# Moving score tile 0 out of the shared score banks, and wider planning margins, in a planned attention + FFN kernel

## The chip, the cores and the metric

The kernel runs on one core of one Trainium2 chip. The metric is the device time of one execution in microseconds, less is better. The kernel before takes 1138.29 us (median of 3 runs, 1138.12 to 1141.94).

## The reference

Attention over 8 batches x 8 heads, 576 positions, head dimension 64, with a block-causal mask (blocks of 64: a query sees all keys of its own block and the blocks before it). Its output, put together to 4608 tokens x 512 features, goes through a bilinear FFN without a nonlinearity:

```
scores = where(block(i) >= block(j), q @ k.T / sqrt(D), -1e9)
attn   = softmax(scores);  x = (attn @ v) as [4608, 512]
out    = ((x @ w_a) * (x @ w_b)) @ w_out          # d_ff = 1536
```

All is float32. The kernel gets float32 accuracy out of cheaper products by splitting each operand into a high and a low part and adding three products.

## The kernel before, in words

**The work.** Two heads make a pair, there are 32 pairs (four a batch). Pairs 0 to 9 multiply in plain float32, pairs 10 to 31 with split operands. Of 576 query rows the first 64 join the last 64 in a side tile, the other 512 make four tiles of 128 rows (0 to 3), which see 192, 320, 448 and 512 keys in the products. For each pair the chain is:

- TensorE, scores: C3 (tile 3), C1 (the side tile, then tile 1), C2 (tile 2), C0 (tile 0), at L542. Head 0 lies on partitions 0 to 63, head 1 on 64 to 127, and their products run at the same time.
- VectorE: masking by memset (L576 to L580), the rows' maxima (t3, t4, t1, t2, t0, L568); ScalarE: the exponentials with their sums (e3, e4, e1, e2, e0, one instruction a head, L595).
- VectorE takes the reciprocals (rc), GpSimd multiplies (N, L683), VectorE transposes in blocks of 32 (T, L688) and sixteen DMAs put these in place (D, L739). Pairs 0 to 5 transpose on TensorE instead.
- TensorE multiplies with v: V, 60 matmuls in four steps (L748), into the output sums' bank, and its first 64 columns into a second bank (`av0`). ScalarE copies the sums out (X, L766 and L767), splits them (H, L787), GpSimd makes the low part (S, L791).

When the four pairs of a batch are done, the batch's tokens can go through the FFN, in two halves of 288 tokens each. A half takes 8 groups `ps` of 12 matmuls (L261) for the two first products of four of the twelve slices of d_ff, and 4 groups `pso` of 12 for the output; ScalarE or VectorE empties each group's bank (copy L837, product L841, copy L873). The rest of d_ff is done in later passes with other code (L1160), which takes from about 560 us to the end and has TensorE alone.

**PSUM.** Eight banks: `x` has two (tiles 3 and 2 of a pair, one bank a head), `y` has two (tile 1 with the side tile, then tile 0), `av` one (the output sums), and `mm` is a ring of three that the FFN's groups, `av0` and a few others take in turn (MM = 3): whoever takes a bank waits until the holder three places before it has released it.

**The order.** All instructions of the attention stage are first listed as operations (`Op`, L365) with an engine, an estimated duration, dependencies and a priority key. `plan` (L376) simulates the five engines and writes their instruction streams in the planned order. So an order is fixed when the program is built, and on the chip each engine works through its stream in that order. Attention's operations have keys near their pair's base time, FFN groups have key 1e6: they fill TensorE whenever no attention operation is ready, in pieces of four matmuls. Two constants matter here. Changing between the three kinds of TensorE work (mode 0 FFN, 1 scores, 2 output) is charged SWITCH = 0.1 us (L406). A TensorE operation that needs another engine's result is planned SLACK = 0.3 us after that result's estimated end (L417). Ring banks are followed by `since` (L391) with the holder's planned release and no such margin.

**Around the change.** C3 of a pair waits for e2 of the pair before (bank x), C1 for e0 of the pair before (bank y). C2 follows e3 (bank x), C0 follows C2, e1 and e4 (bank y). V of pair p-2 is made to follow C0 of pair p and then has key 0, ahead of all else (L776 to L780). D of pair p waits for V of pair p-2, which frees the buffer. Pair 0 alone (`single`) already puts its tiles 0 and 2 into ring and output banks.

Of the kernel before, what the change touches and what calls it, by code (L numbers as in the profile page):

```python
# [17 lines left out]
P = 128  # L18
# [12 lines left out]
KB = {"lk": 288, "lq": 320, "lv": 320, "cd": 512, "D": 112, "st": 144, "xd": 288}  # L31
RATE, LATENCY = 250.0, 1.9
SLACK = 0.3
MASKED = 1
SINGLE = 1
K2 = 2
# [6 lines left out]
CONV_KEY = 12.0  # L43
CONV_LO = True
KEEP_UNTIL, KEEP_EVERY = 66.0, 2.5
SWITCH = 0.1
LAGS = {"PE": 0.24, "DVE": 0.14, "Activation": 0.17, "Pool": 0.1, "SP": 2.0}
TOOK = {
# [31 lines left out]
}  # L80
EARLY = 5
# [8 lines left out]
def attention_then_bilinear_ffn(  # L90
# [274 lines left out]
    class Op:  # L365

        def __init__(self, kind, eng, fn, deps=(), at=0.0, key=None, mode=0):
            self.kind = kind
            took, lag, also = TOOK[kind]
            self.eng, self.took, self.fn, self.also, self.mode = eng, took, fn, also, mode  # L370
            self.deps = [d if isinstance(d, tuple) else (d, 0.0) for d in deps if d is not None]
            self.at, self.key, self.lag = at, at if key is None else key, lag
            self.n, self.frees, self.end = len(ops), None, None
            ops.append(self)

    def plan(look=0.0):  # L376
        free = dict.fromkeys(LAGS, 0.0)
        ready = {e: [] for e in LAGS}
        users = [[] for _ in ops]
        left = [len(o.deps) for o in ops]  # L380
        for o in ops:
            for d, plus in o.deps:
                users[d.n].append((o, plus))
            if not o.deps:
                ready[o.eng].append(o)
        out = []
        mode = 0
        bus = 0.0
        held = []

        def since(o):  # L391
            if not o.frees:
                return o.at
            if len(held) < MM:
                return o.at
            r = held[-MM]
            return o.at if r is o else 1e9 if r.end is None else max(o.at, r.end)

        while any(ready.values()):
            t, e = min((max(free[e], min(map(since, q))), e) for e, q in ready.items() if q)  # L400
            o = min((o for o in ready[e] if since(o) <= t + look), key=lambda o: (o.key, o.n))
            t = max(t, since(o))
            if o.frees:
                held.append(o.frees)
            ready[e].remove(o)
            free[e] = t + o.took + (SWITCH if e == PE_ and o.mode != mode else 0)  # L406
            if e == PE_:
                mode = o.mode
            if o.also:
                free[ACT_] = max(free[ACT_], t) + o.also  # L410
            o.start, o.end = t, free[e] + o.lag
            if o.kind in KB:
                bus = max(bus, t + LATENCY - 0.3) + KB[o.kind] / RATE
                o.end = bus + 0.3
            out.append(o)
            for u, plus in users[o.n]:
                u.at = max(u.at, o.end + plus + (SLACK if u.eng == PE_ and e != PE_ else 0))  # L417
                left[u.n] -= 1
                if not left[u.n]:
                    ready[u.eng].append(u)  # L420
        assert len(out) == len(ops)
        return out
# [37 lines left out]
    def got(what, p):  # L460
        return done.get((what, p))

    def attention(p):
# [11 lines left out]
        def add(what, eng, fn, deps=(), off=0.0, kind=None, **kw):  # L475
            deps = [(got(*d[:2]), *d[2:]) if isinstance(d, tuple) else (d,) for d in deps]
            done[what, p] = o = Op(kind or what, eng, fn, [(*d, 0.0)[:2] for d in deps if d[0]], key=B0 + off, **kw)
            return o

        add("lk", SP_, lambda: take(p, "k", S, kT[b, h0:h0 + 2].rearrange("h d s -> (h d) s")),  # L480
# [42 lines left out]
        def bank(x):  # L523
            st[x] = ps_sc.tile([P, 2, 512], F32, tag=x, name=f"{x}{n}_{len(st)}")
            return st[x]

        single = p < SINGLE

        def ring(t, h):
            st[t, h] = ps_mm.tile([P, 512], F32, tag="mm", name=f"s{n}_{t}_{h}")  # L530

        def view(t, h):
            if single and t in (0, 2):
                return st[t, h][:, :nk[t]]
            return st["x" if t in (2, LAST) else "y"][:, h, :nk[t]]

        def scores(t, out):
            qk = products(p, heads[p]["q"], heads[p]["k"])
            for j, (qq, kk) in enumerate(qk):
                for h, r in enumerate(rows):  # L540
                    keys = ends(kk[r]) if t == NT else kk[r, :nk[t]]
                    nc.tensor.matmul(  # L542
                        out[h] if isinstance(out, list) else out[:, h], qq[r, q0[t]:q0[t] + P], keys, start=j == 0,
                        stop=j == len(qk) - 1 and not (masked and t != LAST), skip_group_check=masked)
            if masked and t != LAST:
                for h, r in enumerate(rows):
                    to = out[h] if isinstance(out, list) else out[:, h]
                    to, val = (to, neg[r]) if t == NT else (to[:, nk[t] - BLK:nk[t]], neg[r, BLK:])
                    nc.tensor.matmul(to, who[r], val, start=False, stop=True, skip_group_check=True)
# [4 lines left out]

        def c1():
            y = bank("y")
            scores(NT, y[:, :, side])
            scores(1, y[:, :, :nk[1]])

        add("C3", PE_, lambda: scores(LAST, bank("x")), [("ql", p), ("kl", p), ("e3" if single_next else "e2", p - 1)], 0, at=B0, mode=1, kind=nat + "C3")  # L560
        add("C1", PE_, c1, [("C3", p, -LAGS[PE_]), ("ql2", p), *([("e4", p - 1), ("e1", p - 1)] if single_next else [("e0", p - 1)])], 0.1, mode=1, kind=nat + "C1")

        def tile_small():
            st["nm"], st["rc"] = (apool.tile([P, 2, NT + 1], F32, tag=x, name=f"{x}{n}") for x in ("nm", "rc"))
# [52 lines left out]
        exp_pair(NT, [("nb", p)], 4.5)  # L617
        exp_pair(1, [("t1", p)], 5.5)

        if single:  # L620
            c1_ = ("C1", p, -LAGS[PE_])
            r2 = Op("none", PE_, lambda: ring(2, 0), [(got("C1", p), -LAGS[PE_])], key=B0 + K2)

            def c2():
                ring(2, 1)
                scores(2, [view(2, h) for h in range(2)])

            o2 = add("C2", PE_, c2, [(r2, 0.0), c1_], K2 + .01, mode=1, kind=nat + "C2")
            def c0():
                ring(0, 1)  # L630
                st[0, 0] = ps_sc.tile([P, 512], F32, tag="av", name=f"s{n}_0_0")
                scores(0, [view(0, h) for h in range(2)])

            o0 = add("C0", PE_, c0, [("C2", p, -LAGS[PE_]), ("X", p - 1)], K2 + .1, mode=1, kind=nat + "C0")
            add("t2", DVE_, lambda: [nc.vector.tensor_reduce(st["nm"][:, h, 2:3], view(2, h), axis=AX.X, op=ALU.max, negate=True) for h in range(2)], [("C2", p), ("t3", p)], K2 + 1, kind="u2")
            add("t0", DVE_, lambda: [nc.vector.tensor_reduce(st["nm"][:, h, :1], view(0, h), axis=AX.X, op=ALU.max, negate=True) for h in range(2)], [("C0", p), ("t3", p)], K2 + 1.2, kind="u0")
        else:
            add("C2", PE_, lambda: scores(2, bank("x")[:, :, :nk[2]]), [("e3", p), ("C1", p, -LAGS[PE_])], 7.0, mode=1, kind=nat + "C2")
            add("C0", PE_, lambda: scores(0, bank("y")[:, :, :nk[0]]),
                [("C2", p, -LAGS[PE_]), ("e1", p), ("e4", p)], 7.1, mode=1, kind=nat + "C0")  # L640
            if masked:
                done["m2", p] = got("C2", p)
            else:
                add("m2", DVE_, lambda: mask(2, "x"), [("C2", p)], 8.0)
            add("t2", DVE_, lambda: top(2, st["x"][:, :, :nk[2]]), [("m2", p)], 8.1)
            if masked:
                done["m0", p] = got("C0", p)
            else:
                add("m0", DVE_, lambda: mask(0, "y"), [("C0", p)], 8.2)
            add("t0", DVE_, lambda: top(0, st["y"][:, :, :nk[0]]), [("m0", p)], 8.3)  # L650
        exp_pair(2, [("t2", p)], 9.5)
        exp_pair(0, [("t0", p)], 10.5)
        if single:
            r2.frees, o2.frees, o0.frees = done["e2", p].first, done["e2", p], done["e0", p]

# [118 lines left out]
                v0 = o  # L774
            vs = [("V", p, -LAGS[PE_])]
        if p >= PET + 2:  # L776
            done["V0", p - 2].deps.append((done["C0", p], -LAGS[PE_]))
            for c in range(NCH):
                done[f"V{c}", p - 2].key = 0
        v0.frees = add("X", ACT_, evac, [("V", p), ("S1", p - 2), ("xd", p - 2)], 30)  # L780
        add("xd", SP_, lambda: nc.sync.dma_start(xd[hp * P:(hp + 1) * P, b * S:(b + 1) * S], st["xf"]),
            [("X", p)], 31)
# [775 lines left out]
```

## Time and profile before

| what | value |
|---|---|
| median of 3 runs | 1138.29 us (1138.12 to 1141.94) |
| span of the profiled execution, first to last instruction | 1131.4 us |
| TensorE busy | 1106.5 us, 98% |
| VectorE, ScalarE, GpSimd busy | 867.4, 634.7, 407.0 us |
| mean granted TensorE clock | 0.997 |

The profile's span is that of the instructions alone; the run's time has 6.9 us more around it. PE is TensorE's matmuls, PEld its weight loads. Matmuls are pipelined, so that a row's duration holds the way through the array: what a matmul costs in a stream is the distance from its start to the next one's start. Rows of a timeline read: start in us, duration, engine, source line, operation, out<-in, shape, count, and in brackets idle time of the engine before it with what ended it. In the shapes, `64*128` is a score product (64 rows of the array), `128*64` an output product, `128*128` an FFN product.

### The profile page before, as it was taken

How to read it: one execution, taken by the hardware profiler on the slowest of the kernel's cores; microseconds unless marked ns; L12 is line 12 of the kernel's file. 1: busy time of each engine (PE TensorE's matmuls, PEld its weight loads, DVE VectorE, ACT ScalarE, POOL GpSimd, SP SyncE). 2: the span in 40 equal slices, each digit the busy share in tenths (PEclk: the TensorE clock that was granted, in tenths of full speed). 3: DMA queues.
4: the chain of work that ended last, by engine and by line, in shares of the span. 5: the costliest groups of instructions: out<-in, count | busy, mean ns of one | idle time of the engine just before them, and what ended most of it. 6: DMA issues, size and time to landing. Idle time of an engine off the chain costs nothing.

```text
span 1131.4 us, 23204 instructions
## 1 busy us (share of the span) xinstructions
PE 1106.5 (98%) x8441; PEld 1040.2 (92%) x8441; DVE 867.4 (77%) x1797; ACT 634.7 (56%) x1632; POOL 407.0 (36%) x602
## 2 busy tenths in 40 slices
PE   8899999999999999999999999999999999999998
PEld 5567888899989998999999999999999999999998
DVE  6877878687678777753999997787874867867857
ACT  6877576566666556643465554545543545545532
POOL 4876667566656667551100120211202112022020
PEclk9999999999999999999999999999999999999999
DMA  5542688888777877857242663845669135055151
GB/s 171 156 145 87 168 242 217 226 227 213 205 222 210 223 210 201 240 159 209 90 146 73 181 179 86 215 121 144 181 217 333 37 76 112 17 96 102 26 98 56
DMA packets 78257, 178.74 MB, mean 158 GB/s; under 512 B 13120, under 2 KB 34624, under 8 KB 78144
## 3 DMA queue, kind: packets, MB, share of 16 engines
q1 hardware_dynamic: 65472, 159.95, 47.2%
q0 software_dynamic: 12672, 17.31, 10.2%
q8 instruction: 67, 1.10, 0.4%
q14 instruction: 46, 0.38, 0.1%
HBM read 80.74 MB, written 48.76 MB: 114 GB/s over the span
## 4 chain that ended last, share of the span: by engine, by line
PE 78%; DVE 6%; DMA 5%; ACT 4%; POOL 3%; SPq 3%; issue 2%; DVEq 0%; ACTq 0%; POOLq 0%
PE bank L1160 47%; PE ps L261 13%; PE pso L261 6%; PE av L748 5%; PE x L542 3%; PE y L542 2%; SPq L739 2%; ACT e L595 2%; POOL e L683 1%; DMA at<-bl 1%; DVE bl L688 1%; DMA qr<-qT 1%; DVE nm L568 1%; PE tp L709 1%; DMA kr<-kT 1%
## 5 line engine op out<-in xcount | busy, mean ns | idle before, releaser
L1160 PE MATMUL bank<-xh,wab 128*128 128x384 f32 x1344 | 350.0, 338 | 0.7 <-DVE t L1077 0.7
L1266 POOL DMA_DIRECT2D outT<-pt x88 | 78.0, 1129 | 468.6 <-ACT pt L1413 277.6
L1160 PEld LDWEIGHTS bank<-xh,wab 128*128 128x128 f32 x1344 | 244.7, 187 | 1.4 <-DVE t L1077 1.0
L1160 PE MATMUL bank<-xl,wab 128*128 128x384 f32 x672 | 227.0, 338 | 0.0
L261 PE MATMUL ps<-xh,wab 128*128 128x288 f32 x1024 | 213.9, 298 | 0.4 <-ACT ob L873 0.3
L261 PEld LDWEIGHTS ps<-xh,wab 128*128 128x128 f32 x1024 | 165.8, 188 | 6.4 <-issue 4.3
L683 POOL TENSOR_SCALAR e<-e,rc 128x512 f32<-128x512 f32 (+3 forms) x256 | 152.7, 616 | 45.3 <-DVE rc L663 45.3
L261 PE MATMUL ps<-xl,wab 128*128 128x288 f32 x512 | 153.3, 299 | 0.0
L1160 PEld LDWEIGHTS bank<-xl,wab 128*128 128x128 f32 x672 | 125.9, 187 | 0.0
L1077 DVE TENSOR_TENSOR u<-bank,u 128x384 f32<-128x384 f32 x156 | 86.7, 556 | 48.4 <-PE bank L1160 45.2
L688 DVE STREAM_TRANSPOSE bl<-e 128x512 f32<-128x512 f32 (+1 forms) x208 | 110.2, 582 | 10.4 <-POOL e L683 8.7
L1160 PE MATMUL bank<-hz,wo 128*128 128x384 f32 x612 | 110.0, 334 | 0.0
L1160 PEld LDWEIGHTS bank<-hz,wo 128*128 128x128 f32 x612 | 106.5, 188 | 0.0
L748 PEld LDWEIGHTS av<-at,v 128*64 128x64 f32 x1920 | 92.2, 137 | 10.3 <-issue 5.0
L748 PE MATMUL av<-at,v 128*64 128x128 f32 (+1 forms) x1920 | 97.2, 258 | 3.9 <-DMA at<-bl 2.7
L261 PE MATMUL pso<-hh,wo 128*128 128x288 f32 x480 | 100.9, 298 | 0.0
L261 PEld LDWEIGHTS ps<-xl,wab 128*128 128x128 f32 x512 | 96.1, 188 | 3.8 <-issue 3.2
L1077 DVE TENSOR_TENSOR t<-bank,t 128x384 f32<-128x384 f32 x96 | 53.3, 556 | 40.5 <-ACT t L1203 20.3
L261 PEld LDWEIGHTS pso<-hh,wo 128*128 128x128 f32 x480 | 77.6, 188 | 4.4 <-issue 4.1
L595 ACT ACTIVATE e<-y,nm 128x320 f32<-128x320 f32 (+1 forms) x126 | 60.9, 487 | 28.3 <-DVE nm L568 22.4
L568 DVE TENSOR_REDUCE nm<-x 128x2 f32<-128x1024 f32 (+1 forms) x63 | 72.1, 1145 | 5.7 <-PE x L542 4.5
L849 POOL TENSOR_TENSOR hl<-hf,hh 128x288 fp32r<-128x288 f32 x56 | 46.2, 825 | 84.0 <-ACT hh L845 81.6
(156 smaller groups left out, 2006.6 us busy)
## 6 DMA issues: line engine op xcount, KB each, us to landing
at<-bl SPq DMA_DIRECT2D x416, 112.0 KB, 2.5
xr<-xd SPq DMA_DIRECT2D x48, 384.0 KB, 4.6
outT<-pt POOLq DMA_DIRECT2D x88, 192.0 KB, 6.4
cv<-wab SPq DMA_DIRECT2D x24, 512.0 KB, 5.5
v<-vm SPq DMA_DIRECT2D x32, 320.0 KB, 3.5
xd<-xf SPq DMA_DIRECT2D x32, 288.0 KB, 2.6
outT<-ob SPq DMA_DIRECT2D x64, 144.0 KB, 2.3
wabd<-st SPq DMA_DIRECT2D x8, 896.0 KB, 5.3
```

What stands on the lines that cost most here:

```text
L261: nc.tensor.matmul(ps, w_, d_, start=(i == 0), stop=(i == n - 1))
L542: nc.tensor.matmul(out[h] if isinstance(out, list) else out[:, h], qq[r, q0[t]:q0[t] + P], keys, start=j == 0, stop=j == len(qk) - 1 and n ...
L568: nc.vector.tensor_reduce(st["nm"][:, :, t], view, axis=AX.X, op=ALU.max, negate=True)
L595: nc.scalar.activation(out, src, AF.Exp, bias=bias, accum_out=sm[:, h, t, :1])
L683: nc.gpsimd.tensor_scalar(ev, ev, st["rc"][:, h, t:t + 1], 1.0, op0=ALU.mult, op1=ALU.mult)
L688: nc.vector.transpose(dst, es[h][t].rearrange("p (c g q) -> p c g q", g=NQ, q=QB))
L739: nc.sync.dma_start(st["at"][QB * g:QB * (g + 1), i], bl[QB * i:QB * (i + 1), g])
L748: nc.tensor.matmul(out[d], v[:, h, c], a[:, qs, h, e_], start=start, stop=stop, skip_group_check=True)
L849: nc.gpsimd.tensor_tensor(lo, box2["hf"], f32(hi), op=ALU.subtract)
L1077: return lambda: v.tensor_tensor(o, a, b, op=op)
L1160: nc.tensor.matmul(banks[bk], a, b, start=start and not i, stop=i == 3 * n - 1, skip_group_check=not start)
L1266: do("acc", POOL_, lambda: nc.gpsimd.dma_start(part[o * P:(o + 1) * P, ts], t, accum_op=ALU.add), [name], [("part", o, 2 * tt_ + j)], key= ...
```

## The change

The constants: SWITCH goes from 0.1 to 0.2; a new margin CALM = 0.8 takes the place of SLACK = 0.3 for the operations of pairs from APART = 13 on (V: from pair 11 on). In C1 the order of its two parts is turned round in all pairs: tile 1 first, then the side tile.

From pair 13 on (`apart`):

- tile 0 no longer uses bank y. Head 0's scores go to the output sums' bank `av`, head 1's to a bank of the ring, as pair 0 did. C0 now waits for e3 and C1 of its pair and for X of pair p-3 (which frees `av`), and C2 follows C0, where C0 followed C2.
- the mask and the maxima of tile 0 are one instruction a head, no longer one for both, and are ahead of those of tile 2; e0 is ahead of e2. The ring bank is released by e0.
- C1 (from pair 14 on) waits for e4 and e1 of the pair before, no longer for e0.
- V of pair p-2 waits for e0 of pair p (which frees `av`), where it waited for C0 of pair p; from pair 14 on V of pair p-3 also follows C1 of pair p.

```
+CALM = 0.8
+APART = 13
-SWITCH = 0.1
+SWITCH = 0.2
...
-                u.at = max(u.at, o.end + plus + (SLACK if u.eng == PE_ and e != PE_ else 0))
+                u.at = max(u.at, o.end + plus + (u.slack if u.eng == PE_ and e != PE_ else 0))
...
+            if p >= (APART if what != "V" else APART - 2):
+                o.slack = CALM
...
+        apart = single or p >= APART
...
-            if single and t in (0, 2):
+            if t in ((0, 2) if single else (0,) if apart else ()):
                 return st[t, h][:, :nk[t]]
...
             y = bank("y")
+            scores(1, y[:, :, :nk[1]])
             scores(NT, y[:, :, side])
-            scores(1, y[:, :, :nk[1]])
...
-        add("C1", PE_, c1, [..., *([("e4", p - 1), ("e1", p - 1)] if single_next else [("e0", p - 1)])], ...)
+        add("C1", PE_, c1, [..., *([("e4", p - 1), ("e1", p - 1)] if single_next or p > APART else [("e0", p - 1)])], ...)
...
+        def c0():
+            ring(0, 1)
+            st[0, 0] = ps_sc.tile([P, 512], F32, tag="av", name=f"s{n}_0_0")
+            scores(0, [view(0, h) for h in range(2)])
+
+        def top0():
+            for h in range(2):
+                nc.vector.tensor_reduce(st["nm"][:, h, :1], view(0, h), axis=AX.X, op=ALU.max, negate=True)
+
+        def mask0():
+            for h in range(2):
+                nc.vector.memset(view(0, h)[:BLK, nk[0] - BLK:], NEG)
...
+            if apart:
+                o0 = add("C0", PE_, c0, [("e3", p), ("C1", p, -LAGS[PE_]), ("X", p - 3)], 6.9, mode=1, kind=nat + "C0")
+            add("C2", PE_, lambda: scores(2, bank("x")[:, :, :nk[2]]), [("e3", p), ("C1", p, -LAGS[PE_]), *([("C0", p, -LAGS[PE_])] if apart else [])], 7.0, mode=1, kind=nat + "C2")
+            if not apart:
+                add("C0", PE_, lambda: scores(0, bank("y")[:, :, :nk[0]]),
+                    [("C2", p, -LAGS[PE_]), ("e1", p), ("e4", p)], 7.1, mode=1, kind=nat + "C0")
...
+            elif apart:
+                add("m0", DVE_, mask0, [("C0", p)], 7.8, kind="mm0")
+                add("t0", DVE_, top0, [("m0", p)], 7.9, kind="u0")
...
+        if apart and not single:
+            exp_pair(0, [("t0", p)], 9.4)
         exp_pair(2, [("t2", p)], 9.5)
-        exp_pair(0, [("t0", p)], 10.5)
+        if not apart or single:
+            exp_pair(0, [("t0", p)], 10.5)
+        if apart and not single:
+            o0.frees = done["e0", p]
...
-            done["V0", p - 2].deps.append((done["C0", p], -LAGS[PE_]))
+            done["V0", p - 2].deps.append((done["e0", p], 0.0) if apart else (done["C0", p], -LAGS[PE_]))
...
+        if p > APART:
+            done["V0", p - 3].deps.append((done["C1", p], -LAGS[PE_]))
```

More of the change, by code (lines that the diff above doesn't have):

```diff
@@ L372, in __init__ @@
             self.at, self.key, self.lag = at, at if key is None else key, lag
-            self.n, self.frees, self.end = len(ops), None, None
+            self.n, self.frees, self.end, self.slack = len(ops), None, None, SLACK
             ops.append(self)
@@ L556, in c1 @@
             y = bank("y")
+            scores(1, y[:, :, :nk[1]])
             scores(NT, y[:, :, side])
-            scores(1, y[:, :, :nk[1]])
         add("C3", PE_, lambda: scores(LAST, bank("x")), [("ql", p), ("kl", p), ("e3" if single_next else "e2", p - 1)], 0, at=B0, mode=1, kind=nat + "C3")
-        add("C1", PE_, c1, [("C3", p, -LAGS[PE_]), ("ql2", p), *([("e4", p - 1), ("e1", p - 1)] if single_next else [("e0", p - 1)])], 0.1, mode=1, kind=nat + "C1")
+        add("C1", PE_, c1, [("C3", p, -LAGS[PE_]), ("ql2", p), *([("e4", p - 1), ("e1", p - 1)] if single_next or p > APART else [("e0", p - 1)])], 0.1, mode=1, kind=nat + "C1")
         def tile_small():
@@ L626, in c2 @@
                 scores(2, [view(2, h) for h in range(2)])
[L628 to L632, printed above, removed]
+            o2 = add("C2", PE_, c2, [r2, c1_], K2 + .01, mode=1, kind=nat + "C2")
             o0 = add("C0", PE_, c0, [("C2", p, -LAGS[PE_]), ("X", p - 1)], K2 + .1, mode=1, kind=nat + "C0")
             add("t2", DVE_, lambda: [nc.vector.tensor_reduce(st["nm"][:, h, 2:3], view(2, h), axis=AX.X, op=ALU.max, negate=True) for h in range(2)], [("C2", p), ("t3", p)], K2 + 1, kind="u2")
-            add("t0", DVE_, lambda: [nc.vector.tensor_reduce(st["nm"][:, h, :1], view(0, h), axis=AX.X, op=ALU.max, negate=True) for h in range(2)], [("C0", p), ("t3", p)], K2 + 1.2, kind="u0")
+            add("t0", DVE_, top0, [("C0", p), ("t3", p)], K2 + 1.2, kind="u0")
         else:
-            add("C2", PE_, lambda: scores(2, bank("x")[:, :, :nk[2]]), [("e3", p), ("C1", p, -LAGS[PE_])], 7.0, mode=1, kind=nat + "C2")
-            add("C0", PE_, lambda: scores(0, bank("y")[:, :, :nk[0]]),
-                [("C2", p, -LAGS[PE_]), ("e1", p), ("e4", p)], 7.1, mode=1, kind=nat + "C0")
+            if apart:
[4 more added lines that the diff above has]
+                    [("C2", p, -LAGS[PE_]), ("e1", p), ("e4", p)], 7.1, mode=1, kind=nat + "C0")
             if masked:
@@ L647, in attention @@
                 done["m0", p] = got("C0", p)
+            elif apart:
+                add("m0", DVE_, mask0, [("C0", p)], 7.8, kind="mm0")
+                add("t0", DVE_, top0, [("m0", p)], 7.9, kind="u0")
             else:
                 add("m0", DVE_, lambda: mask(0, "y"), [("C0", p)], 8.2)
-            add("t0", DVE_, lambda: top(0, st["y"][:, :, :nk[0]]), [("m0", p)], 8.3)
+            if not apart:
+                add("t0", DVE_, lambda: top(0, st["y"][:, :, :nk[0]]), [("m0", p)], 8.3)
+        if apart and not single:
+            exp_pair(0, [("t0", p)], 9.4)
         exp_pair(2, [("t2", p)], 9.5)
-        exp_pair(0, [("t0", p)], 10.5)
+        if not apart or single:
+            exp_pair(0, [("t0", p)], 10.5)
+        if apart and not single:
+            o0.frees = done["e0", p]
         if single:
```

1 row of the table TOOK is left out of this document.

## The prediction

> **What bounds the kernel now.** I read the page first, then busy time by stretch, then TensorE's timeline in the stretch that the change touches, then who waits for whom there.
>
> ```profile
> span 1131.4 us, 23204 instructions
> ...
> PE 1106.5 (98%) x8441; PEld 1040.2 (92%) x8441; DVE 867.4 (77%) x1797; ACT 634.7 (56%) x1632; POOL 407.0 (36%) x602
> ```
> ```profile
> 0.00:195.70 195.70, 180.82 (x1623) 142.08 (x1623) 153.93 (x334) 139.26 (x431) 132.59 (x214) 0.98 0.57 170
> 195.70:494.20 298.50, 295.16 (x3003) 269.84 (x3002) 225.87 (x526) 187.06 (x597) 181.87 (x280) 1.00 0.77 212
> ```
>
> TensorE bounds it. The second window row is the stretch from C3 of pair 13 to the last V before the tail; its columns are length, busy PE, PEld, DVE, ACT, POOL, clock, DMA share, GB/s. TensorE has work in 295.16 of 298.50 us at clock 1.00, since FFN groups fill whatever attention leaves. So a shorter attention chain by itself is worth nothing here; only what TensorE itself loses counts. It loses in two ways, waits and changes between kinds of work. The changes are seen in starts, not in busy time:
>
> ```profile
> 394.10 0.86 PE L542 MATMUL x<-k,q 64*128 64x448 f32 x6
> 394.89 0.40 PE L261 MATMUL pso<-hl,wo 128*128 128x288 f32 x1
> ...
> 396.96 0.29 PE L261 MATMUL pso<-hl,wo 128*128 128x288 f32 x1
> 397.19 0.58 PE L542 MATMUL y<-k,q 64*128 64x192 f32 x6
> 397.70 2.98 PE L748 MATMUL av<-at,v 128*64 128x64 f32 x60
> 400.61 0.96 PE L542 MATMUL x<-k,q 64*128 64x512 f32 x6
> 401.41 0.94 PE L542 MATMUL y<-k,q 64*128 64x128 f32 x12
> 402.28 0.54 PE L261 MATMUL pso<-hh,wo 128*128 128x288 f32 x2
> 402.65 0.29 PE L261 MATMUL pso<-hl,wo 128*128 128x288 f32 x1
> ...
> 405.42 0.29 PE L261 MATMUL pso<-hl,wo 128*128 128x288 f32 x1
> ```
>
> From 402.65 to 405.42 lie 21 FFN matmuls, so one costs 0.132 us in a stream. The stretch between C2 and C0 (394.89 to 397.19, sixteen matmuls) takes 2.30 us where 16 x 0.132 is 2.11: 0.19 us go to entering and leaving it. C2 costs 0.79 (394.10 to 394.89), C0 0.51, V 2.91, C3 with C1 1.67.
>
> **The change part by part.** *C0 and C2 side by side.* Apart, they and the stretch's overhead cost 0.79 + 0.19 + 0.51 = 1.49 us. Where the planner happened to put them together, the row reads:
>
> ```profile
> 471.77 0.88 PE L542 MATMUL x<-k,q 64*128 64x448 f32 x6
> 472.48 0.47 PE L542 MATMUL y<-k,q 64*128 64x192 f32 x6
> 472.89 0.40 PE L261 MATMUL ps<-xl,wab 128*128 128x288 f32 x1
> ```
>
> 1.12 us from 471.77 to 472.89, so 0.37 us less. Of the 19 pairs from 13 on, 17 are apart now (394.10 is one) and 2 together (472.48 and one at 490.18). In the changed plan C0 has every dependency of C2 and one more, and C2 only adds C0, so nothing fits between them. 17 x 0.37 = **6.3 us less**. The order inside the block (192 columns before 448) and inside C1 I cost at nothing: the number of matmuls and columns is the same; the side tile's maxima come after tile 3's on VectorE, which hides the later side tile.
>
> *V moves from behind C0 to behind C1.* In the rows above V starts at 397.70 behind C0 and C3 follows it at 400.61; the new place is behind C1, at 402.28, 4.6 us later. An entry from the FFN is saved in the nine pairs in which V now starts from a stretch, and lost in the nine in which V now runs straight on into C3, as it does here: 9 x 0.19 each way, 0. X, H, S and xd go with V, and so does D two pairs on (it needs V's buffer), in SP's queue. The cover is older FFN work:
>
> ```profile
> 400.73 0.59 ACT L767 COPY xf<-av 128x512 f32<-128x512 f32 x1 [0.92 <-PE av L748]
> ```
> ```profile
> 402.41 0.82 POOL L791 TENSOR_TENSOR xl<-xf,xh 128x288 fp32r<-128x288 f32 x1
> ```
> ```profile
> 425.40 0.40 PE L261 MATMUL ps<-xl,wab 128*128 128x288 f32 x1
> ...
> 426.56 0.29 PE L261 MATMUL pso<-hh,wo 128*128 128x288 f32 x1
> ```
>
> This V is pair 23's, the last of its batch; its low part is there at 403.2. The batch's FFN begins 24 matmuls ahead of the outputs at 426.56, which by the streams between is about 419.4. So 16 us of cover stand against 4.6; if it were gone, TensorE would idle for the difference once a batch, in the four batches of pairs 12 to 27.
>
> *Wider margins* (0.5 us more on every wait for another engine, and 0.1 us more for each change of work). What they can remove is what TensorE still waits for:
>
> ```profile
> PE x L542 <- ACT e L595: 2.0, 3, 1.4
> PE av L748 <- PE av L748: 1.1, 2, 0.7
> ```
> ```profile
> 321.47 0.96 PE L542 MATMUL x<-k,q 64*128 64x512 f32 x6 [1.36 <-ACT e L595]
> ```
> ```profile
> 507.36 2.87 PE L748 MATMUL av<-at,v 128*64 128x128 f32 x56 [0.92 <-DMA at<-bl]
> ...
> 519.78 2.87 PE L748 MATMUL av<-at,v 128*64 128x128 f32 x56 [1.14 <-DMA at<-bl]
> ```
>
> The first two rows are waits of 195.7 to 494.2 us (total, times, longest). A margin of 0.5 us takes 0.5 off the 1.36 and all of the other 0.6 of that row, about 1.0 of the second row, and 0.5 off each of the last two: 3.1 us at most, 0 if new waits of the same kind appear elsewhere in the new order. I take **2.5 us less**, since a wider margin works wherever they appear. Its price is attention that starts later, which the FFN fills.
>
> *More work on VectorE*: one memset and one reduction more a pair.
>
> ```profile
> L568 DVE TENSOR_REDUCE nm<-y 128x2 f32<-128x384 f32 x19 | 10.6, 557 | 0.5
> L568 DVE TENSOR_REDUCE nm<-y 128x2 f32<-128x256 f32 x19 | 7.9, 415 | 0.4
> L580 DVE MEMSET y<- 64x128 f32 x38 | 6.3, 165 | 4.9 <-ACT a L837 1.0 <-ACT ob L873 1.0 <-PE y L542 0.7
> ```
>
> 128 columns are worth 142 ns between these two reductions, so one of 192 is about 0.35 us (an estimate) and two are 0.15 us over the present 0.557; with a memset of 0.165 that is 0.31 us a pair, 6 us in all on an engine that is busy for 225.87 of 298.50 us. Hidden, 0.
>
> *A ring bank for C0, and C0 behind X.* C0 now holds a ring bank until e0, and waits for X, a copy of 0.59 us on ScalarE behind V. No row shows either. A gain is excluded, as both only add a condition to TensorE. The lower end is 0: after C0 and C2 (1.12 us) two FFN groups of 12 x 0.132 = 1.58 us can run in the other two banks, so e0 has 4.3 us from C0's start. The upper end is the rival below. How long C0 to e0 takes now:
>
> ```profile
> 410.36 0.58 PE L542 MATMUL y<-k,q 64*128 64x192 f32 x6
> ```
> ```profile
> 399.51 0.20 ACT L595 ACTIVATION_READ_ACCUMULATOR e<-y,nm 128x1 f32 x1
> ...
> 414.83 0.74 ACT L504 ACTIVATE q<-qr 128x640 fp32r<-128x640 f32 x1 [1.09 <-DMA qr<-qT]
> ...
> 416.18 0.20 ACT L595 ACTIVATION_READ_ACCUMULATOR e<-y,nm 128x1 f32 x1
> ```
>
> 2.5 us for the C0 at 397.19, 6.0 us for that at 410.36, where e0 stands behind e2 and behind the next pair's q, which waits for a DMA. The change puts e0 ahead of e2, so I take the shorter row as nearer and charge 0.1 us a pair, **1.9 us more**. The Trainium skill, page "TensorEngine Tiling (Array Packing)", section "Gotcha 1: PSUM Pressure", speaks against this part: row tiles need banks of their own, so the tile takes two banks from the FFN and the sums; no run here shows that price yet.
>
> *SWITCH before pair 13.* It changes the plan of the first 195.70 us, where TensorE idles for 14.9 us. Any other order there may gain or lose some of that; I take 0 and allow 3 us both ways, a fifth of it.
>
> Sum against the profiled execution: 1131.4 - 6.3 - 2.5 + 1.9 = 1124.5 us. The median of the runs is 6.9 us over that profile's span, so **1131.4 us**. A difference of 0.5% (5.7 us, or a time of 1132.6) is about what a measurement of this kernel can tell from none.
>
> **The rivals.** *The waits come back* (same): the joins bring 6.3 us, but C0 waits for X and the ring about as long, 0.2 to 0.3 us a pair (4 to 6 us), and the margin gives nothing: 1136 to 1138. For it: two new conditions on TensorE; against it: 0.5 us more margin on the first of them. That the change does nothing at all is not open, since the joining follows from the dependencies.
>
> *The ring starves the FFN* (slower): e0 keeps standing behind the next pair's q on ScalarE, the third group after C0 finds no bank, and TensorE stops from 4.3 us after C0 until e0. At the 6.0 us of the second row that is 1.7 us; in half of the 19 pairs 16 us: 1138.3 - 8.8 + 16 = 1145.5. It decides from the point at which e0 comes more than 4.3 us after C0. For it: the planner gives ring banks no margin; against it: e0's new place. This is the skill's gotcha as a time.
>
> *More than forecast* (faster): the first stage gains its 3 us as well and the ring costs nothing: 1126.5.
>
> **How the numbers follow.** Forecast 0.60, its own range 1127.5 to 1135.8 (all 3.1 us of waits, no ring price and half of the first stage's 3 us at one end; no margin gain and the ring's price doubled at the other), three quarters of it below 1132.6. Waits come back 0.22, ring starves 0.10, more than forecast 0.08. Faster by over 0.5%: 0.45 + 0.07 = 0.52. Slower by over 0.5%: 0.10. Same: 0.38. The range 1126 to 1141 leaves out most of the starving case and the ends of the others.
>
> **What would show it.** Right: in TensorE's timeline from 210 us on only two entries a pair, C3 C1 V and C0 C2, the latter 1.1 us long; no bracket of over 0.5 us before C0, C3 or an FFN group. Wrong: FFN stretches that end in waits for e0 or X; idle time before `ps` or `pso` that did not exist; a first stage (to C3 of pair 13) that ends more than 3 us from 195.7.

## The result, and the profile after

The changed kernel takes 1143.20 us (median of 8 runs, 1141.22 to 1147.68). The kernel before takes 1136.76 us over its 8 runs (1132.28 to 1141.94), five of them new. The ratio is 1.0060, with an interval of 1.0039 to 1.0082: slower, by some 6.4 us, where 1131.4 us and a gain were forecast.

The page of the changed kernel, span and busy time:

```profile
span 1143.4 us, 23201 instructions
...
PE 1104.8 (97%) x8441; PEld 1043.7 (91%) x8441; DVE 871.1 (76%) x1835; ACT 629.6 (55%) x1632; POOL 407.4 (36%) x602
```

TensorE has 1.7 us less to do than before (1106.5) and is idle for 13.7 us more. The next views cut the spans at C3 of pair 13 and at the first matmul of the later passes (out `bank`). Columns as before: stretch, length, busy PE, PEld, DVE, ACT, POOL, clock, DMA share, GB/s. First the changed kernel, then the middle stage of the kernel before:

```profile
0.00:202.10 202.10, 180.70 (x1619) 143.42 (x1619) 151.42 (x329) 137.77 (x428) 130.98 (x210) 0.98 0.56 164
202.10:594.10 392.00, 379.93 (x3728) 357.40 (x3728) 288.33 (x695) 222.05 (x689) 198.47 (x304) 1.00 0.70 196
594.10:1143.40 549.30, 544.17 (x3098) 542.89 (x3096) 431.38 (x812) 269.79 (x519) 77.94 (x88) 1.00 0.48 125
```
```profile
195.70:583.30 387.60, 381.86 (x3723) 355.34 (x3723) 282.99 (x654) 226.54 (x685) 196.37 (x301) 1.00 0.71 198
```

Before pair 13 the same work takes 202.10 us instead of 195.70, and TensorE idles there for 21.4 us (202.10 - 180.70) instead of 14.9. In the middle stage it idles for 12.1 us (392.00 - 379.93) instead of 5.7. The passes behind it hardly differ (549.3 against 548.1).

The joins came as forecast. Two pieces of TensorE's timeline in the changed kernel, around C0 with C2 of one pair (out `s` and `x`) and around C3, C1 and V behind it:

```profile
244.11 0.29 PE L264 MATMUL pso<-hh,wo 128*128 128x288 f32 x1
244.33 0.58 PE L548 MATMUL s<-k,q 64*128 64x192 f32 x6
244.75 0.80 PE L548 MATMUL x<-k,q 64*128 64x448 f32 x6
245.48 0.40 PE L264 MATMUL ps<-xh,wab 128*128 128x288 f32 x1
...
251.42 0.96 PE L548 MATMUL x<-k,q 64*128 64x512 f32 x6
252.21 0.89 PE L548 MATMUL y<-k,q 64*128 64x320 f32 x12
253.03 2.99 PE L774 MATMUL av<-at,v 128*64 128x64 f32 x60
255.95 0.40 PE L264 MATMUL ps<-xl,wab 128*128 128x288 f32 x1
```

C0 with C2 takes 1.15 us (244.33 to 245.48), and only two entries from the FFN are left a pair. Counted over the middle stage, TensorE changes its kind of work 133 times before and 99 times after; 34 changes fewer are 17 stretches of FFN less; at the prediction's 0.37 us a join that is 6.3 us.

Only 1.9 us of it are left in the middle stage's busy time (381.86 to 379.93), for which "What stays open" has the account. What the stage loses beside that is in TensorE's waits from 202 to 530 us of the changed kernel (total us, times, longest; the rows of 1.0 us or more):

```profile
PE ps L264 <- ACT e L601: 3.8, 3, 3.4
PE ps L264 <- DVE hf L869: 2.4, 2, 1.3
PE ps L264 <- ACT a L865: 1.9, 3, 1.3
PE pso L264 <- ACT a L865: 1.0, 1, 1.0
PE x L548 <- ACT e L601: 1.0, 2, 0.7
```

The first four rows are FFN groups without a ring bank, 9.1 us; with a smaller row of 0.4 us it is 9.5. The kernel before had a single wait of that kind from 195.7 us on:

```profile
PE ps L261 <- ACT ob L873: 0.3, 1, 0.3
```

Attention's own waits (`x`, `y`, `av`) have become few. Measured from the start of C0 to the end of e0's second exponential (its read of the sum comes 0.1 us later), the 19 pairs have a median of 4.57 us, 13 of them above the prediction's 4.3 us. So at first sight the rival "the ring starves the FFN" has come true, and its 1145.5 us is near. The experiments say otherwise.

### The profile page after: what moved, and what is told of

Its sections match the earlier page's. It is cut to its first block, busy times and chain, and to the rows that moved or that the text cites. A ratio compares the mean times of both kernels' runs of the same rounds, so it can differ in the third digit from the quotient of the medians.

```text
span 1143.4 us, 23201 instructions
## 1 busy us (share of the span) xinstructions
PE 1104.8 (97%) x8441; PEld 1043.7 (91%) x8441; DVE 871.1 (76%) x1835; ACT 629.6 (55%) x1632; POOL 407.4 (36%) x602
## 4 chain that ended last, share of the span: by engine, by line
PE 62%; DVE 11%; ACT 10%; DMA 6%; POOL 5%; issue 3%; SPq 3%; ACTq 0%; DVEq 0%; POOLq 0%
PE bank L1188 47%; PE ps L264 6%; ACT e L601 4%; PE av L774 4%; POOL e L709 3%; DMA qr<-qT 3%; PE pso L264 3%; SPq L765 2%; DVE nm L574 2%; PE x L548 2%; DMA kr<-kT 1%; DVE q L513 1%; DMA at<-bl 1%; PE y L548 1%; ACT q L509 1%
## 5 line engine op out<-in xcount | busy, mean ns | idle before, releaser
L264 PE MATMUL ps<-xh,wab 128*128 128x288 f32 x1024 | 216.3, 300 | 8.8 <-ACT e L601 3.8
L601 ACT ACTIVATE e<-y,nm 128x320 f32<-128x320 f32 (+1 forms) x88 | 45.2, 514 | 94.0 <-POOL e L709 41.5
L819 POOL TENSOR_TENSOR xl<-xf,xh 128x288 fp32r<-128x288 f32 x62 | 51.2, 829 | 59.3 <-ACT xh L815 54.3
```

The costliest lines, as they stand in the source:

```text
L264: nc.tensor.matmul(ps, w_, d_, start=(i == 0), stop=(i == n - 1))
L601: nc.scalar.activation(out, src, AF.Exp, bias=bias, accum_out=sm[:, h, t, :1])
L819: (nc.vector if p == NP - 1 else nc.gpsimd).tensor_tensor(lo, st["xf"][:, j * HT:(j + 1) * HT], f32(hi), op=ALU.subtract)
```

## The experiments

Three explanations stood at first: the ring bank that C0 holds too long; SWITCH, which changes the order of the whole plan; and the wider margin, which puts attention off. Every kernel was timed in five rounds beside the kernel before on the same chip, whose median was 1135.8 to 1137.6 us in these batches. "Stages" below are the three stretches above, in one profiled execution. One caution for them: e3 and e15 to e18 have the same planned order up to pair 13, and their first stage took 194.9, 198.1, 198.3, 200.2 and 197.3 us. A difference of 3 us in one profile's first stage is therefore nothing. And e3's profile is of its fastest run (1126.08 us), the changed kernel's of one 2.0 us above its median, so the stage differences between these two add up to 19.1 us where the medians differ by 13.6.

**One part at a time.** SWITCH alone, in the kernel before:

```
-SWITCH = 0.1
+SWITCH = 0.2
```

> The kernel before with one number changed: SWITCH 0.2 for 0.1. Theory A (the larger charge for a change of work reorders pairs 0 to 12 and this order is worse on the chip): C3 of pair 13 starts at about 202 us instead of 195.7, and the time is 4 to 7 us over the kernel before (ratio about 1.005). Rival (the turned order inside C1, or scatter between executions): C3 of pair 13 within 2 us of 195.7 and the time within 2 us.

1161.83 us, ratio 1.0205 (1.0178 to 1.0233): this one constant costs the kernel before 24 us, over three times what either side expected. Its stages are 204.0, 407.4 and 548.1 us, so the loss is larger behind pair 13 than before it, and there it has nothing to do with the ring's new holder, which this kernel lacks. TensorE's largest waits from 200 to 530 us:

```profile
PE x L542 <- ACT e L595: 8.3, 11, 2.4
PE x L542 <- ACT q L504: 3.2, 3, 1.5
PE av L748 <- DMA at<-bl: 2.5, 2, 1.8
```

Here it is attention's own waits that grew. The order inside C1 alone, in the kernel before (tile 1 ahead of the side tile):

```
+            scores(1, y[:, :, :nk[1]])
             scores(NT, y[:, :, side])
-            scores(1, y[:, :, :nk[1]])
```

> The kernel before with only the two parts of C1 turned round (tile 1 first, then the side tile). Theory A: no difference, within 2 us, and C3 of pair 13 at 195.7 within 2 us. Rival (the later side tile delays t4, nb and e3 in every pair): 4 to 7 us over the kernel before, C3 of pair 13 at about 202 us.

1135.86 us, ratio 0.9987 (0.9970 to 1.0005): no difference. The opposite test, the whole change but for SWITCH:

```
-SWITCH = 0.2
+SWITCH = 0.1
```

> The changed kernel with SWITCH back at 0.1; all else of the change stays. Theory A: the first stage is as before (C3 of pair 13 at 196 within 2 us) and the time falls by 5 to 7 us from the changed kernel, to the kernel before within 3 us. Rival (C1's order, or the bank change itself, is what costs): it stays 5 us over the kernel before.

1129.63 us (9 runs, 1126.08 to 1134.49), ratio 0.9936 (0.9915 to 0.9956). Without the one constant the change gains 8.0 us (1137.64 to 1129.63), and it is 13.6 us faster than the change as made. That is more than either expectation allowed. Its stages, and its waits of 0.4 us or more from 190 to 530 us:

```profile
0.00:194.90 194.90, 178.72 (x1623) 143.06 (x1623) 155.07 (x334) 138.76 (x430) 132.98 (x215) 0.99 0.57 170
194.90:575.00 380.10, 375.18 (x3723) 354.49 (x3723) 284.00 (x691) 220.94 (x684) 198.20 (x299) 1.00 0.73 202
575.00:1124.30 549.30, 544.21 (x3098) 542.93 (x3096) 431.58 (x812) 269.65 (x520) 77.83 (x88) 1.00 0.49 125
```
```profile
PE pso L264 <- ACT a L865: 2.4, 5, 0.6
PE av L774 <- DMA at<-bl: 1.3, 1, 1.3
PE x L548 <- ACT q L509: 0.7, 1, 0.7
PE x L548 <- ACT e L601: 0.4, 1, 0.4
```

In the middle stage TensorE is busy for 375.18 us where the kernel before needs 381.86: 6.7 us, the joins. Idle are 4.9 us. The changes of work are 99, as many as in the change as made. So from pair 13 on SWITCH = 0.2 brought not one join more, and only cost.

**The margin.** SWITCH and the wider margin on everything, in the kernel before:

```
-SLACK = 0.3
+SLACK = 0.8
-SWITCH = 0.1
+SWITCH = 0.2
```

> The kernel before with SWITCH 0.2 and SLACK 0.8 for all pairs; the banks stay as before. Theory C (with 0.1 us a change TensorE is planned too fast, falls behind its plan on the chip, and that lateness is the margin in which the other engines' results arrive; 0.2 takes it away): the wider margin gives it back, TensorE's waits from pair 13 on fall from the 17 us of the SWITCH-only kernel to 8 or less and the time from 1162 to 1150 or less. Rival D (the plan at 0.2 is a worse order, margin or not): over 1157.

1165.96 us, ratio 1.0250 (1.0218 to 1.0283): the margin doesn't heal what SWITCH does. The margin as the change has it, alone in the kernel before:

```
+CALM = 0.8
+APART = 13
...
+            if p >= (APART if what != "V" else APART - 2):
+                o.slack = CALM
```

> The kernel before with only the margin of 0.8 us from pair 13 on (V from 11); SWITCH 0.1 and the banks as before. By the prediction's second term 2.5 us less than before (1135), changes of work on TensorE as before (133 from pair 13 on). Rival (the margin brings the gain): 6 to 8 us less, 1130.

1136.27 us, ratio 0.9987 (0.9966 to 1.0007): nothing that can be measured. And the change with the old SWITCH and the old margin:

```
-CALM = 0.8
+CALM = 0.3
-SWITCH = 0.2
+SWITCH = 0.1
```

> The changed kernel with SWITCH 0.1 and CALM 0.3 (the old margin): the bank change and C1's order alone. Theory C: SWITCH 0.1 is most of the margin needed; waits from pair 13 on are 1 to 4 us over the 4.7 us of the kernel with SWITCH 0.1 and CALM 0.8, time 1130 to 1134. Rival (the 0.8 us margin, not the banks, brings the gain): 1136 to 1139, as the kernel before.

1131.73 us, ratio 0.9963 (0.9939 to 0.9986), beside e3's 0.9936 (0.9915 to 0.9956). The margin may be worth the 2 us between them; the intervals overlap. It isn't the cause of the loss.

**How the time depends on SWITCH.** In the changed kernel, only the constant differs: 0.0, 0.11 and 0.15.

```
-SWITCH = 0.2
+SWITCH = 0.0      # e8; 0.11 in e9, 0.15 in e10
```

> The changed kernel with SWITCH 0.0. Theory C: even more lateness of TensorE, so waits no higher than with 0.1, and time 1126 to 1132. Rival D (the charge picks a lucky or an unlucky order): anywhere from 1125 to 1145, with C3 of pair 13 moved by more than 3 us.

> The changed kernel with SWITCH 0.11. Theory S (the loss grows with the charge, because TensorE's work is planned later): a tenth of the 13.6 us between 0.1 and 0.2, so 1130 to 1132. Theory O (the charge only tips which of two nearly equal operations the planner takes first, and the order found at 0.1 happens to suit the chip): not in proportion, 3 us or more above 1131 or below 1128.

> The changed kernel with SWITCH 0.15. Theory S: half way, 1135 to 1138. Theory O: anywhere between 1128 and 1150, with no regard to the order 0.1, 0.11, 0.15, 0.2.

In the order 0.0, 0.1, 0.11, 0.15, 0.2 the medians are 1145.52, 1129.63, 1135.39, 1136.27 and 1143.20 us, the ratios of the three new ones 1.0080 (1.0052 to 1.0108), 0.9994 (0.9974 to 1.0015) and 0.9996 (0.9978 to 1.0014). It is no price that grows with the constant: 0.01 us of charge costs 5.8 us, and no charge at all costs as much as 0.2. Theory S has the time of 0.15 right, but not those of 0.11 and 0.0. One could also think that 0.1 is what the chip pays, since the prediction's 0.19 us for entering and leaving an FFN stretch are two changes; but 0.11 is as near to that. So the constant doesn't act by its size alone. The reading that is left is that it tips decisions of a plan that takes the best operation at each moment, that every later decision follows from the earlier ones, and that 0.1 happens to come out well; no run shows a single such decision. At 0.0 the waits are of yet another kind (from 200 to 560 us):

```profile
PE x L548 <- ACT e L601: 9.8, 4, 3.8
```

**Where the loss is made.** SWITCH is 0.2 until the planner has placed C3 of pair 13, and 0.1 from there on (e11), or the other way round (e12):

```
+        switch, turn = SWITCH, done["C3", APART]
...
-            free[e] = t + o.took + (SWITCH if e == PE_ and o.mode != mode else 0)
+            free[e] = t + o.took + (switch if e == PE_ and o.mode != mode else 0)
+            if o is turn:
+                switch = SWITCH_LATE
```

> The changed kernel with SWITCH 0.2 until C3 of pair 13 is planned and 0.1 from there on. If the loss is made in each stage by its own order: C3 of pair 13 at 202 us, some 7 us over the kernel with 0.1 throughout, 1135 to 1138, and ring waits of under 5 us after it. Rival (the first stage's delay is worked off later by the FFN): 1131 or less.

> The changed kernel with SWITCH 0.1 until C3 of pair 13 is planned and 0.2 from there on. If the loss is made in each stage by its own order: C3 of pair 13 at 195 us, and some 6 us over the kernel with 0.1 throughout, 1134 to 1137, with C0 to e0 over 4.3 us in most pairs and TensorE waiting for ring banks for 6 us or more. Rival (only the first stage matters): 1131 or less.

1135.38 us (ratio 0.9987, 0.9970 to 1.0004) and 1139.18 us (1.0022, 1.0006 to 1.0038). Against e3's 1129.63 that is 5.8 us for the early part and 9.6 us for the late one, together 15.4 where the whole costs 13.6. The loss is made in both stages, more of it behind pair 13. The program's own plan has C3 of pair 13 at 182.2 us with 0.1 (e3, e12) and at 189.3 us with 0.2 (the change as made, e11). That looks like the early loss, but the plan charges 87 changes of work before this C3 with 0.1 and 78 with 0.2, so that 8.7 and 15.6 us are charge: 6.9 of the 7.1 us. Without its charges the plan has the two orders equally long up to there (within 0.2 us), and the loss shows on the chip alone.

**Is the ring the cause, or a symptom?** The late kernel e12 has a C0 to e0 of 5.05 us (median), and ring waits from 194 to 575 us like those of the change as made:

```profile
PE ps L264 <- ACT e L604: 6.5, 4, 3.0
PE ps L264 <- ACT a L868: 2.6, 2, 1.4
```

First attempts to part the two moved e0. In the change as made (e4) and with SWITCH at 0.1 (e13), the next pair's casts of k and q on ScalarE are planned behind e0; in e14, with SWITCH at 0.1, e0 is planned behind the next q.

```
-            add("kh", ACT_, kh, [("lk", p)], -12)
+            add("kh", ACT_, kh, [("lk", p), *([("e0", p - 1)] if p > APART else [])], -12)
...
-            add("qh", ACT_, qh, [("lq", p)], -12)
+            add("qh", ACT_, qh, [("lq", p), *([("e0", p - 1)] if p > APART else [])], -12)
```
```
+            if p > APART:
+                done["e0", p - 1].first.deps.append((done["qh", p], 0.0))
```

> The changed kernel, and from pair 14 on the next pair's k and q casts on ScalarE are planned behind e0 of the pair. Theory B (FFN groups stop for ring banks because e0, the copies and the products behind it stand in their queues behind casts that wait for a DMA): TensorE's waits before ps and pso, 9.5 us in the changed kernel from 202 to 530 us, fall to under 4 us, the 3.4 us wait at 493 is gone, and the time falls by 4 to 7 us from the changed kernel. Rival (three banks are too few whatever the order): these waits stay within 2 us of 9.5.

> The changed kernel with SWITCH 0.1 and the next pair's k and q casts planned behind e0. If the hold of C0's ring bank is all that this moves: C0 to e0 at 2.2 us in most pairs, ring waits from 2.3 us to under 1, time 1127 to 1130. Rival (later casts lengthen each pair, the FFN's stock runs out at the ends of batches as it did with SWITCH 0.2): TensorE waits of 2 to 3 us in each fourth pair between C0 and C2, time 1138 to 1146.

> The changed kernel with SWITCH 0.1 and the opposite order: e0 is planned behind the next pair's q cast in every pair from 13 on. Ring theory: C0 to e0 is over 4.3 us in 15 or more of 19 pairs, TensorE's waits for ring banks rise from 2.3 us to 6 us or more, and the time by 4 to 10 us to 1134 to 1140. Rival (three banks suffice, and the ring waits with SWITCH 0.2 have another cause): ring waits of under 4 us, time within 3 us of 1130.

e4: 1146.59 us, ratio 1.0090 (1.0065 to 1.0116). C0 to e0 falls from 4.57 to 2.19 us, the waits for the ring are down to 0.2 us, and the time does not fall. Its largest wait from 202 to 560 us:

```profile
PE x L548 <- ACT e L601: 10.4, 4, 2.6
```

This is C2 waiting for e3, every fourth pair, with no FFN group to fill the gap: the FFN's stock ran out before the next batch's was there, and the ring's wait was replaced by one as long. e13 shows the same beside e3: ring waits down to 0.2 us, 1135.90 us against 1129.63, ratio 0.9994 (0.9975 to 1.0013). e14 hardly moved the median of e0 (3.70 us against 3.69) and took 1129.49 us, ratio 0.9943 (0.9919 to 0.9967); it tells nothing apart. All three also moved other work, so a cleaner test was needed: hold the bank longer and move nothing. In e15 a copy of one column on VectorE (0.15 us) reads C0's ring bank behind e2 and e0; e16 is the same behind e0 alone.

```
+            def hold():
+                nc.vector.tensor_copy(apool.tile([P, 1], F32, tag="hold", name=f"hold{n}"), view(0, 1)[:, :1])
+
+            add("hold", DVE_, hold, [("e2", p), ("e0", p)], 10.6, kind="none")
```

> The changed kernel with SWITCH at 0.1 (1129.6 us), in which one tiny copy of 128x1 on VectorE, for each pair from 13 on, reads score tile 0's bank of the FFN's ring after e2 and e0, so that the bank comes free later; the planned orders of the other engines are as they were. Theory (the late release of the ring's bank is what costs): the FFN's waits for the ring rise from 2.3 us to 6 to 10 us, and the time to 1134 to 1141 us. Rival (the order of work costs, and the bank's late release is a symptom): waits for the ring under 4 us, and the time within 3 us of 1130.

> The same tiny copy right behind e0 alone, as a control for what the copy itself costs: both theories expect 1130 us within 2 us, and waits for the ring of 2 to 3 us.

1129.01 us (ratio 0.9924, 0.9895 to 0.9952) and 1130.64 us (0.9937, 0.9915 to 0.9958). The bank came free 4.68 and 4.83 us after C0 (medians), in 14 and 16 of 19 pairs later than 4.3 us. That is as late as in the change as made (4.57 us, 13 pairs), but the ring waits near C0 were 2.2 and 3.4 us and not 9.5. Between themselves the two held the bank equally long, so the control controlled nothing. The last two kernels go further. In both, the copy stands behind the first multiplication by the reciprocals; e17's reads the bank, e18's reads the reciprocals. The order of all five engines is e3's but for the copy, and e17 and e18 differ only in what it reads and in what follows from that: which of the three banks each FFN group gets.

```
+                if i == h == 0 and apart and not single:
+                    add("hold", DVE_, lambda: nc.vector.tensor_copy(apool.tile([P, 1], F32, tag="hold", name=f"hold{n}"),
+                        view(0, 1)[:, :1]), [prev], 13.5, kind="none")     # e18: st["rc"][:, 0, :1]
```

> As e15, but the tiny copy that reads score tile 0's ring bank stands in VectorE's stream behind the first multiplication by the reciprocals, which the plan has 6.5 to 7.0 us after C0; all five planned orders are otherwise those of the changed kernel with SWITCH at 0.1. Theory (a ring bank that comes free late stops the FFN): the FFN's waits for the ring rise from 2.3 us by up to 19 x (6.9 - 4.3) = 49 us, by half of it (25 us) if half of the pairs have a third FFN group there, so that the time comes to 1145 to 1175 us. Rival (the order of work costs, the ring's release doesn't): waits for the ring under 5 us and the time within 3 us of the control.

> The same tiny copy at the same place in VectorE's stream, reading the reciprocals instead of the bank: the bank comes free with e0. Both theories expect 1130 us within 3 us and waits for the ring of 2 to 3 us; what e17 takes above this is the price of the late release alone.

1131.73 us (ratio 0.9957, 0.9942 to 0.9972) and 1129.55 us (0.9946, 0.9926 to 0.9966). In e17 the bank comes free 7.25 us after C0, in all 19 pairs later than 4.3 us. Waits of TensorE of 0.3 us or more from 190 to 545 us, e17 first:

```profile
PE ps L264 <- ACT a L867: 2.5, 3, 1.2
PE av L776 <- DMA at<-bl: 2.1, 1, 2.1
PE pso L264 <- ACT a L867: 1.5, 3, 0.5
PE pso L264 <- POOL hl L879: 0.6, 1, 0.6
PE ps L264 <- DVE hf L871: 0.5, 2, 0.3
PE pso L264 <- DVE hold L753: 0.3, 1, 0.3
```
```profile
PE pso L264 <- ACT a L867: 2.8, 4, 1.5
PE av L776 <- DMA at<-bl: 1.8, 1, 1.8
PE pso L264 <- POOL hl L879: 0.6, 1, 0.6
PE x L548 <- ACT e L601: 0.4, 1, 0.4
PE ps L264 <- ACT xf L794: 0.3, 1, 0.3
```

Only one wait, of 0.3 us, ends with the copy that holds the bank. Without the `hl` rows, which are a wait for data, the FFN's ring waits are 4.8 us against 3.1. Between the medians are 2.2 us, with intervals that overlap; even from the outer end of one to that of the other it is 5 us. The theory asked for 1145 us at least. So the late release by itself costs some 2 us when all 19 pairs have it, and cannot be the 9.6 us of the late part.

Why it costs so little is in the program. "The kernel before" has the ring's banks taken strictly in turn; that is how the planner counts, but the built program doesn't do so. In 18 of e17's 19 pairs 36 to 52 FFN matmuls stand between C2 and C3, three groups and more, and they hardly wait: the groups pass C0's bank by and use the other two in turn, and in 4 pairs only a group asks for C0's bank before C3. In e18 this happens in 18 pairs. So e17 doesn't show that a group which does ask for a late bank goes on unhindered.

In the changed kernel some do ask. All of its ring waits end 3.7 to 7.9 us after the start of a C0, and all but one of 0.2 us end while e0 still holds C0's bank or within 0.5 us of its release; e3's five waits for the copy `a` end 4.3 to 5.2 us after one, but are 0.2 to 0.6 us long. 3.8 of the 9.5 us end with e0 itself, nearly all in one wait of 3.4 us; the other rows end with the FFN's own emptying copies and products. With SWITCH at 0.1 the same bank in the same ring costs 2.4 us, so the order of work decides what the ring costs. Which swap in ScalarE's and VectorE's streams does it was not settled, and no run keeps the changed kernel's order and gives C0's bank back earlier.

The fastest version is the change with SWITCH left at 0.1 (e3, 1129.63 us); e14, e15, e16 and e18 are variants of it within 1.1 us of that.

## Why the prediction was wrong

**The step that failed** is "SWITCH before pair 13": "I take 0 and allow 3 us both ways, a fifth of it". It was wrong in place and in size. SWITCH orders all of the plan, not the first stage alone: 9.6 us of its loss lie behind pair 13 (e12), 5.8 before it (e11). And it costs 13.6 us in the changed kernel and 24 in the kernel before (e1). The bound was a fifth of the first stage's idle time, as if a new order could only move what is idle now; an order that fits the chip less well makes waits that the trace of before doesn't hold. That the loss comes from this constant is shown (e3, e1); why this order is the worse one is open.

**Without that step the sum holds.** The other edits were summed to -6.3 - 2.5 + 1.9 = -6.9 us; e3 has -8.0 us against the kernel before beside it, and its 1129.6 us is 1.8 us from the forecast. Without the margin the sum is -4.4, and e6 has -5.4.

- *C0 and C2 side by side, 6.3 us less*: right. TensorE's busy time in the middle stage fell by 6.7 us in e3, and a block takes 1.15 us where 1.12 was forecast. Of the 6.7 us, spacing of scores and outputs has 5.2 (56.8 to 53.1 and 62.7 to 61.2). C1's order at nothing: right (e2).
- *V behind C1, at nothing*: no row of waits in the changed kernel or e3 ends with GpSimd's low part of X, so the cover held at V's new place. The entries saved and lost are part of the 34 above.
- *Margins, 2.5 us less*: not shown. Alone they give nothing that can be measured (e7), though the interval doesn't exclude 2.5 us; in the changed order perhaps 2 us (e6 beside e3).
- *VectorE, at nothing*: right as far as seen; of TensorE's waits in e3 none ends with a maximum or a mask.
- *Ring and X, 1.9 us more*: e3's ring waits near C0 sum to 2.4 us, so the size was near. The threshold was not right: e17 passes 4.3 us in every pair and loses some 2 us. A third FFN group does follow at once, but it can use a bank that one of the first two has given back, since the banks are not handed out strictly in turn.
- *The rival with the ring* named the time (1145.5) and the sign, and its signs are in the trace of the change (9.5 us of ring waits). Its chain, e0 behind the next pair's q and a third group that waits for C0's bank, is there in full once, in the 3.4 us wait shown below. But it had this in half of the pairs at 1.7 us, for 16 us. And e0 past 4.3 us isn't enough to make it: in e17 the bank is late in every pair and the time stays. That the rival's number is near is luck.
- *6.9 us around the span*: wrong as a reading. The changed kernel's profiled run took 1145.17 us with a span of 1143.4, so 1.8 us lie outside. With as much outside, the span of 1131.4 was that of an execution of some 1133 us, at the lower end of before's runs (1132.28 to 1141.94). It did the forecast no harm, since the sum went by differences.

**What stays open.** The change's middle stage is 11.9 us longer than e3's. Idle time accounts for 7.2 of it (12.1 - 4.9), nearly all of that ring waits (9.5 against 2.4), the half clock below for 1.7; some 3 us of longer spacing, most of it in the FFN's streams, have no owner.

## What to carry to other kernels

A constant of a planner that writes the whole order is not a small edit: 0.01 us of charge moved this kernel by 5.8 us, so such a constant is changed and timed by itself, and in a forecast it gets the widest bound of all, with both signs. A wait that grows in the profile beside a slower time is not yet the cause; a test that makes the wait's condition worse and leaves every order alone (e17 beside e18) tells more than moving the suspect operation, which only trades one wait for another (e4, e13). Even then it pays to look at what else the program does differently, here the banks. And where a profile has one execution, its span is compared with the time of its own run, not with the median of the others.

## What the runs showed of the hardware

One wait costs more than its length. The longest wait of the changed kernel, in TensorE's and ScalarE's timelines:

```profile
489.76 0.29 PE L264 MATMUL ps<-xh,wab 128*128 128x288 f32 x1
493.46 0.40 PE L264 MATMUL ps<-xh,wab 128*128 128x288 f32 x1 [3.40 <-ACT e L601]
```
```profile
487.75 0.68 ACT L517 CAST k<-kr 128x576 fp32r<-128x576 f32 x1 [1.77 <-DMA kr<-kT]
...
491.86 0.74 ACT L509 ACTIVATE q<-qr 128x640 fp32r<-128x640 f32 x1 [1.89 <-DMA qr<-qT]
492.51 0.40 ACT L601 ACTIVATE e<-s,nm 128x192 f32<-128x192 f32 x1
...
493.30 0.40 ACT L865 COPY a<-ps 128x288 f32<-128x288 f32 x1
```

An FFN group waits for the ring bank that e0 holds; e0 stands on ScalarE behind the next pair's casts of k and q, which wait 1.77 and 1.89 us for their DMAs. The copy `a` that empties the FFN's own bank stands behind e0, so that bank was no earlier to be had. Then the granted clock (the column behind the five engines) by stretches of 3.4 us:

```profile
490.60:494.00 3.40, 0.54 (x4) 0.55 (x5) 1.37 (x2) 1.83 (x6) 0.15 (x1) 1.00 0.65 162
494.00:497.40 3.40, 3.40 (x16) 3.40 (x16) 1.29 (x5) 2.63 (x8) 1.78 (x3) 0.50 0.75 174
497.40:500.80 3.40, 3.40 (x38) 3.03 (x38) 2.00 (x4) 0.43 (x1) 3.11 (x5) 1.00 0.45 104
```

Behind the wait TensorE runs at half clock for 3.4 us, which costs another 1.7 us. Over all profiles, between 200 and 560 us, 17 of the 21 waits from 1.6 to 3.8 us have such a stretch that begins in the wait or at most 2 us behind it (the shortest is e2's of 1.61 us), and none of the 15 between 1.2 and 1.6 us has. But length alone doesn't decide: in e13, waits of 1.10 us with one of 0.8 us shortly before them have it in two of four cases. The Trainium skill, page "TensorE: Matmul & The Clock Gate", section "HAM oscillation — how this bites in real kernels", gives the rule that gaps over about 3.4 us are to be avoided; here, in e2, less than half of that was enough.
